# Sink-and-window attention with top-1 experts: packed score chunks, on-chip routing and 16 fixed expert blocks

## The chip, the cores and the metric

One core of one Trainium2 chip. The metric is device microseconds of one execution; the medians are over the runs shown. The profile is of one execution.

## The reference

Attention over 4 batches, 8 heads, 768 positions of 64 numbers. Heads 0, 2 and 6 (`retr` below) see all earlier positions, the other five ("streaming") the last 64 and the first 4 ("sinks"). The result, 3072 rows of 512, goes row by row through a layer of 8 experts: a row whose product with `w_skip` is positive goes to the expert with the largest logit, and its gated output is added to the row; every other row is left as it is.

```python
scores = np.where(mask[None, :, :, :], scores, -1000000000.0)
a = np.exp(scores - np.max(scores, axis=-1, keepdims=True))
attn = np.matmul(a / (np.sum(a, axis=-1, keepdims=True) + 1e-09), v)
...
do_compute = x @ w_skip > 0
e_idx = np.argmax(xc @ w_gate, axis=1)
h = np.maximum(xc[mask] @ w1[e], 0.0)
y[mask] = gate_w[mask, None] * (h @ w2[e])
out[do_compute] = xc + y
```

## The kernel before

It runs in four stages, and a framework orders each engine's instructions and sets the waits from what they read and write.

*Attention* (lines 162 to 327) loops over batches and pairs of heads. POOL's queue loads q, k and v head by head, cast to f16 on the way, in pieces of 64 numbers (lines 172, 174, 197). TensorE transposes q and k of a pair (lines 180, 184); ScalarE and VectorE copy them to `qT` and `kT`. Scores are computed transposed, keys on the partitions, 128 keys and up to 512 queries at a time with 64 rows of the array (line 217), into one PSUM bank of two; each goes through one exponential (line 223) and, where it touches a mask's edge, a VectorE product (lines 226, 249). A streaming head takes 128 keys by 256 queries, and its sinks are a strip of 4 rows. P·V (line 268) puts all six query tiles of a head in one PSUM tile, with a column of ones in V for the sum; lines 275 and 276 divide. After a batch the rows go to DRAM (`attn_x`), are transposed in fp32 (line 289), and multiplied by the gate's matrix (line 297); one row block of 128 at a time is turned into a gate weight and a one-hot row (lines 302 to 327).

*Routing* (lines 333 to 421) starts after the last batch: ranks by a triangular matmul, 24 indirect writes of row numbers to eight DRAM shards (line 404), a load of the shards, and a minimum over them.

*Experts* (lines 441 to 501): each expert has 384 slots, as 256 and 128, whatever its rows. Per expert POOL issues two weight loads, and per 128 slots a gather of rows (line 456) and of gate weights (line 463). VectorE scales, TensorE transposes in fp32 (line 472), then the up matmuls (line 481), one ReLU (line 488) and the down matmuls (line 493); the result goes to DRAM by slot.

*Return* (lines 503 to 518): per 128 rows an indirect load by slot (line 510), a sum and a store.

```python
          nc.gpsimd.dma_start(out=w1t, in_=w1r[e])
          nc.gpsimd.dma_start(out=w2t, in_=w2r[e])
          for mt in CHSZ:
            for s2 in range(nsm):
                nc.gpsimd.indirect_dma_start(
                    out=xg, out_offset=None, in_=X[:, :],
```

## Time and profile before

| | us |
|---|---|
| median of 3 runs (502.64 to 507.01) | 503.84 |
| profiled execution, first to last instruction | 499.5 |
| attention, 0 to 225 | 225 |
| routing, 225 to 281 | 56 |
| experts, 281 to 450 | 169 |
| return, 450 to 499.5 | 49.5 |

The profiled execution's own time is its span and the start and end around it, which the profile doesn't show; the median lies 4.3 us above the span. Engines are PE (TensorE), PEld (its weight loads), DVE (VectorE), ACT (ScalarE), POOL (GpSimd) and SP. A matmul's end is modelled; its start is recorded. The stages are told apart by which lines run.

### The profile page before, as it was taken

To read this page: it belongs to the slowest core of one execution; us is meant where nothing else is said; L and a number is where in the kernel's file an instruction comes from. 1 tells how busy PE (TensorE), PEld (TensorE's weight loads), DVE (VectorE), ACT (ScalarE), POOL (GpSimd) and SP (SyncE) were. 2 spreads that over 40 slices of the span, in tenths; PEclk is the share of its full clock that TensorE was granted. 3 is DMA by queue.
4 is the path that set the end of the run, shared out by engine and by line. 5 is a ranking of instruction groups with operands and counts; after the bars stand their busy time and mean duration, and the time that the engine had idled before them with its cause. 6 is when DMAs were issued, how large, how long until landed. Compare 5 with 4: busy or idle time off the path is not lost.

```text
span 499.5 us, 6050 instructions
## 1 busy us (share of the span) xinstructions
PE 313.7 (63%) x1981; PEld 175.0 (35%) x1981; DVE 208.8 (42%) x883; ACT 135.2 (27%) x317; POOL 202.8 (41%) x269
## 2 busy tenths in 40 slices
PE   0699999998999999962000048766868668770000
PEld 0344454444444444331000035534535444540000
DVE  1245566455654665467000134141441423316563
ACT  1464646564645564610000002101111012020000
POOL 9976751553011100000674636342533525005662
PEclk9999999999999999999999999979699798896555
DMA  4999991999132511031000694959679589512675
GB/s 31 120 103 88 82 202 11 70 65 173 11 25 18 142 10 8 2 126 2 1 0 9 112 206 112 170 126 206 122 162 168 122 162 183 125 52 95 211 229 184
DMA packets 108207, 50.51 MB, mean 101 GB/s; under 512 B 85079, under 2 KB 93671, under 8 KB 108176
## 3 DMA queue, kind: packets, MB, share of 16 engines
q0 software_dynamic: 94240, 31.04, 54.1%
q10 hardware_dynamic: 6000, 10.59, 6.0%
q1 hardware_dynamic: 7936, 8.51, 5.0%
q8 instruction: 15, 0.25, 0.2%
q14 instruction: 16, 0.13, 0.1%
HBM read 65.14 MB, written 19.00 MB: 168 GB/s over the span
## 4 chain that ended last, share of the span: by engine, by line
PE 45%; DMA 22%; issue 9%; POOL 9%; DVE 7%; ACT 6%; ACTq 0%; POOLq 0%; SPq 0%; DVEq 0%
DMA xg<-attn_x,merged 14%; PE pst L217 13%; PE opsa L268 10%; PE yps L493 6%; PE hps L481 5%; PE gxtp L289 4%; ACT ats L223 3%; ACT ht L488 2%; POOL fyg L510 2%; DMA fyg<-y_sorted,slot_i 2%; DMA gw<-gate_w,merged 2%; POOL sorted_sh L404 2%; PE qTps L180 2%; PE kTps L184 2%; DMA sorted_sh<-row_idx,slot_i 2%
## 5 line engine op out<-in xcount | busy, mean ns | idle before, releaser
L223 ACT ACTIVATE ats<-pst 128x256 f16<-128x256 f32 (+4 forms) x236 | 92.6, 417 | 74.1 <-PE pst L217 71.8
L217 PE MATMUL pst<-qT,kT 64*128 64x256 f16 (+4 forms) x236 | 91.0, 426 | 3.8 <-ACT ats L223 1.0
L488 ACT ACTIVATE ht<-hps 128x2048 f16<-128x2048 f32 (+1 forms) x16 | 23.2, 1450 | 196.8 <-PE hps L481 134.2
L268 PE MATMUL opsa<-va,ats 128*128 128x65 f16 x552 | 69.8, 241 | 2.9 <-ACT ats L223 2.3
L197 POOL DMA_DIRECT2D va<-in_v_dram x32 | 26.7, 843 | 94.0 <-PE opsa L268 54.5
L493 PE MATMUL yps<-w2t,ht 128*128 128x512 f16 x192 | 52.8, 433 | 18.7 <-ACT ht L488 18.7
L268 PEld LDWEIGHTS <-ats 128*128 128x128 f16 x552 | 41.3, 117 | 54.7 <-DVE ats L226 12.2
L481 PE MATMUL hps<-xTm,w1t 128*128 128x128 f16 (+1 forms) x512 | 48.0, 255 | 1.0 <-DVE xTm L475 1.0
L404 POOL DMA_INDIRECT sorted_sh<-row_idx,slot_i x24 | 23.4, 977 | 57.2 <-DVE slot_i L398 50.2
L481 PEld LDWEIGHTS <-w1t 128*128 128x128 f16 x512 | 42.0, 102 | 10.4 <-issue 3.8
L510 POOL DMA_INDIRECT fyg<-y_sorted,slot_i x24 | 26.5, 1104 | 42.2 <-DVE fyg L509 37.7
L472 PE MATMUL xtp<-identf,xg 128*128 128x128 f32 x96 | 18.9, 351 | 36.2 <-DVE xg L468 36.2
L468 DVE TENSOR_SCALAR xg<-xg,gw 128x512 f32<-128x512 f32 x24 | 11.4, 492 | 67.8 <-DMA xg<-attn_x,merged 52.2
L493 PEld LDWEIGHTS <-ht 128*128 128x128 f16 x192 | 19.2, 107 | 47.2 <-ACT ht L488 23.2
L456 POOL DMA_INDIRECT xg<-attn_x,merged x24 | 24.8, 1033 | 22.4 <-issue 19.0
L217 PEld LDWEIGHTS <-kT 64*128 64x128 f16 (+1 forms) x236 | 20.5, 102 | 27.8 <-issue 16.2
L289 PE MATMUL gxtp<-identf,xsb 128*128 128x128 f32 x96 | 29.3, 435 | 0.9 <-DVE xsb L276 0.9
L174 POOL DMA_DIRECT2D kin<-in_k_dram x32 | 27.8, 867 | 3.8 <-PE kTps L184 2.6
L172 POOL DMA_DIRECT2D qin<-in_q_dram x32 | 27.7, 866 | 3.0 <-PE pst L217 2.0
L475 DVE CAST xTm<-xtp 128x512 f16<-128x512 f32 x24 | 15.8, 681 | 30.7 <-PE xtp L472 30.7
L180 PE MATMUL qTps<-ident,qin 128*128 128x128 f16 x96 | 18.8, 308 | 14.9 <-DMA qin<-in_q_dram 14.9
L472 PEld LDWEIGHTS xtp<-identf,xg 128*128 128x128 f32 x96 | 14.7, 181 | 37.8 <-DVE xg L468 20.6
(111 smaller groups left out, 369.1 us busy)
## 6 DMA issues: line engine op xcount, KB each, us to landing
w1t<-in_moe_w_dram POOLq DMA_DIRECT2D x8, 1024.0 KB, 9.4
w2t<-in_moe_w_dram POOLq DMA_DIRECT2D x8, 1024.0 KB, 12.3
y_sorted<-ys ACTq DMA_DIRECT2D x16, 256.0 KB
qin<-in_q_dram POOLq DMA_DIRECT2D x32, 96.0 KB, 3.3
kin<-in_k_dram POOLq DMA_DIRECT2D x32, 96.0 KB, 3.3
va<-in_v_dram POOLq DMA_DIRECT2D x32, 96.0 KB, 3.2
attn_x<-xsb SPq DMA_DIRECT2D x12, 256.0 KB
attn_x<-xsb ACTq DMA_DIRECT2D x12, 256.0 KB
```

What stands on the lines that cost most here:

```text
L174: nc.gpsimd.dma_start(out=kin[:, :, hd, :], in_=kv[b, h0 + hd].transpose([1, 0, 2]))
L180: nc.tensor.matmul(qTps[:, n * P:(n + 1) * P], qin[:, n].rearrange("p h d -> p (h d)"), ident, is_transpose=True, start=(n == 0), stop=(n ...
L217: nc.tensor.matmul(pst[:k_rows, :qn], kTh[:, j * P:j * P + k_rows], qTh[:, q_lo:q_hi], start=True, stop=True)
L223: nc.scalar.activation(dst, pst[:k_rows, :qn], ACT.Exp)
L268: nc.tensor.matmul(opsa[:, i, :], ats[:kr, sl, i * QB:i * QB + QB], vh[:kr, j, :], start=(cnt == 1), stop=(cnt == total))
L289: nc.tensor.matmul(xtp[:, s, :], xc[:, s * P:(s + 1) * P], identf, is_transpose=True, start=(s == 0), stop=(s == DS - 1))
L404: nc.gpsimd.indirect_dma_start(out=SH[c % NSHARD][:, None], out_offset=bass.IndirectOffsetOnAxis(ap=slot_i[:, c:c + 1], axis=0), in_=row_i ...
L472: nc.tensor.matmul(xtp[:, s, :], xg[:, s * P:(s + 1) * P], identf, is_transpose=True, start=(s == 0), stop=(s == DS - 1))
L481: nc.tensor.matmul(hps[:, fs, :mt], w1t[:, s, fs * P:(fs + 1) * P], xT[:, s, :mt], start=(s == 0 and fs % BPB == 0), stop=(s == DS - 1 and ...
L488: nc.scalar.activation(ht[:, :, :mt], hps[:, :, :mt], ACT.Relu)
L493: nc.tensor.matmul(yps, ht[:, fs, s2 * P:(s2 + 1) * P], w2t[:, fs, :], start=(fs == 0), stop=(fs == FS - 1))
L510: nc.gpsimd.indirect_dma_start(out=yg, out_offset=None, in_=YS[:, :], in_offset=bass.IndirectOffsetOnAxis(ap=slot_i[:, c:c + 1], axis=0), ...
```

## The change

The kernel is written anew. What it does:

- q and k are loaded whole per batch (only batch 0 in parts), 384 numbers a piece, so position 6p + n lies on partition p; v by tiles of 128 positions. All of it is issued by POOL, and so are the weights: batches 0 and 1 and expert 0 at the start, then one batch and one expert a round, with buffers for five experts.
- `trans` transposes each head apart, onto output rows 0 to 63 or 64 to 127. `retr` packs the lower triangle of a retrieval head into three chunks of up to 1024 columns, each with one exponential. `strm` packs a streaming head's window into one tile of 768 columns, keys 0 to 63 of each tile on the upper half and 64 to 127 on the lower, the lower shifted by 64. `sinks` computes the sink scores of five heads in one tile of 20 rows.
- `prep_v` copies V on POOL so that the shifted tiles find theirs. `avx` does P·V for one query tile of all heads, divides, stores the rows to the output itself, and makes the logits from an f16 cast by POOL.
- The scores of batch b stand beside `avx` of batch b - 1, one query tile at a time (`front`, `NF` and the loop at line 486).
- `route` turns a batch's logits into ranks, and by one-hot matmuls into a table with row number and gate of each of 256 slots of each expert, without DRAM; the gate is carried in three f16 parts.
- The experts have 2 blocks of 128 slots. All 16 gathers read the output, up to 128 rows each; the result is added to the gathered rows and scattered back to the output (line 581). After that the largest count is read into the engines' registers; if it is over 256, a loop does the further blocks with weights loaded again (lines 604 to 671).

```diff
+    def load_qk(b, split):
+        q_in[b] = qkp.tile([P, H, NT * D], FP16, tag="qin", name="qin")
...
+    def load_v(b):
+        va[b] = vp.tile([P, NT, H, V1], FP16, tag="va", name="va")
+        for i in range(NT):
+            nc.gpsimd.dma_start(out=va[b][:, i, :, :D], in_=vr[b, i])
...
+    load_qk(0, True)
+    load_v(0)
...
+    load_qk(1, False)
+    load_v(1)
+    load_w(0)
...
+    sp = att.enter_context(tc.tile_pool(name="sp", bufs=2, space=PSUM))
+    tp = att.enter_context(tc.tile_pool(name="tp", bufs=2, space=PSUM))
+    ap_ = att.enter_context(tc.tile_pool(name="ap", bufs=1, space=PSUM))
...
+    def prep_v(b):
+        nc.gpsimd.memset(va[b][:, :, :, D:], 1.0)
+        vs[b] = vsp.tile([P, NT, 5, V1], FP16, tag="vs", name="vs")
+        for dst, src in ((slice(0, 4), slice(1, 8, 2)), (slice(4, 5), slice(4, 5))):
+            nc.gpsimd.tensor_copy(vs[b][:D, :, dst], va[b][:D, :, src])
+            nc.gpsimd.tensor_copy(vs[b][D:, 1:, dst], va[b][D:, :NT - 1, src])
...
+    def trans(b, pr):
+        for name, src, dst in (("qT", q_in[b], qT), ("kT", k_in[b], kT)):
+            ps = tp.tile([P, NT, P], FP16, tag="t", name="tps")
+            for n in range(NT):
+                for i, h in enumerate(PAIRS[pr]):
+                    nc.tensor.matmul(ps[i * D:(i + 1) * D, n],
+                                     src[:, h, n * D:(n + 1) * D], ident,
+                                     is_transpose=True, start=(n == 0),
+                                     stop=(n == NT - 1))
...
+    CH = (((0, 0, 0, 512), (0, 512, 512, 256), (4, 512, 768, 256)),
+          ((1, 128, 0, 512), (1, 640, 512, 128), (3, 384, 640, 384)),
+          ((2, 256, 0, 512), (5, 640, 512, 128)))
+    CHO = ((0, 1024, 768), (1024, 1024, 640), (2048, 640, 512))
...
+        for j, q0, o, w in CH[c]:
+            for i in heads:
+                r = slice(i * D, (i + 1) * D)
+                nc.tensor.matmul(ps[i][:, o:o + w], kT[b, pr][r, j * P:(j + 1) * P],
+                                 qT[b, pr][r, q0:q0 + w], start=True, stop=True)
...
+    def strm(b, pr, i):
...
+        ps = sp.tile([P, 1024], FP32, tag="s", name="sps")
+        for n in range(NT):
+            c = n * P
+            nc.tensor.matmul(ps[:D, c:c + P], kt[r, c:c + D], qt[r, c:c + P],
+                             start=True, stop=True)
+            lo, hi = (0 if n == 0 else c + D), min(c + D + P, S)
+            for x, y in (((lo, 512), (512, hi)) if lo < 512 < hi else ((lo, hi),)):
+                nc.tensor.matmul(ps[D:, x:y], kt[r, c + D:c + P], qt[r, x:y],
+                                 start=True, stop=True)
...
+        nc.scalar.activation(a, ps[:, :S], ACT.Exp, scale=SCALE)
+        nc.vector.tensor_tensor(a, a, smask.rearrange("p i c -> p (i c)"), op=ALU.mult)
...
+    def avx(b, i):
...
+        x = xp.tile([P, 4, 2, D], FP32, tag="x", name="x")
+        for t in range(2):
+            o = ap_.tile([P, 4, V1], FP32, tag=f"av{t}", name=f"av{t}")
+            nc.tensor.matmul(o, esk[b % 2][:, i * P:(i + 1) * P], vsk[:, b, t],
+                             start=True, stop=False)
+            for c in range(4):
+                h = 2 * c + t
+                a = at[b, h]
+                fin = c == 3
+                if h in RETR:
+                    for j in range(i + 1):
+                        x0 = COL[j] + (i - j) * P
+                        nc.tensor.matmul(o[:, c], a[:, x0:x0 + P], va[b][:, j, h],
+                                         start=False, stop=fin and j == i)
+                else:
+                    u = SINKS.index(h) if h != 4 else 4
+                    q0 = i * P
+                    nc.tensor.matmul(o[:D, c], a[:, q0:q0 + D], vs[b][:, i, u],
+                                     start=False, stop=fin)
+                    nc.tensor.matmul(o[D:, c], a[:, q0 + D:q0 + P], va[b][:, i, h],
+                                     start=False, stop=fin)
+            rec = tiny.tile([P, 4], FP32, tag=f"rec{t}", name="rec")
+            nc.vector.reciprocal(rec, o[:, :, D])
+            nc.vector.tensor_tensor(x[:, :, t], o[:, :, :D],
+                                    rec.unsqueeze(2).to_broadcast([P, 4, D]), op=ALU.mult)
+        xf = x.rearrange("p c t d -> p (c t d)")
+        (nc.sync if i % 2 else nc.scalar).dma_start(out=outr[b, i], in_=xf)
+        x16 = xp.tile([P, DM], FP16, tag="x16", name="x16", bufs=2)
...
+    def route(b):
...
+        for i in range(NT):
+            ol = tiny.tile([P, P], FP16, tag="ol", name="ol", bufs=4)
+            nc.vector.tensor_scalar(ol, iota16, lo[:, i:i + 1], None, ALU.is_equal)
+            nc.tensor.matmul(tb, ol, mv[:, i], start=(i == 0), stop=(i == NT - 1))
...
+    for b in range(B + 1):
+        steps = list(front(b)) if b < B else []
+        if b < B:
+            prep_v(b)
+        for i in range(NT):
+            if b:
+                avx(b - 1, i)
+            for f in steps[i * len(steps) // NT:(i + 1) * len(steps) // NT]:
+                f()
+        if b:
+            route(b - 1)
+        if b + 2 < B:
+            load_qk(b + 2, False)
+            load_v(b + 2)
+        if b + 1 < NW and b < B:
+            load_w(b + 1)
+    att.close()
...
+        def gather(e):
...
+                sl = t * E + e
+                xg[e, t] = mxp.tile([P, DM], FP32, name=f"xg{e}_{t}")
+                nc.vector.memset(xg[e, t], 0.0)
+                nc.gpsimd.indirect_dma_start(
+                    out=xg[e, t], out_offset=None, in_=out[:, :],
+                    in_offset=bass.IndirectOffsetOnAxis(ap=idx[:, sl:sl + 1], axis=0),
+                    bounds_check=N - 1, oob_is_err=False)
+        for e in range(3):
+            gather(e)
+        load_w(NW)
+        for e in range(3, E):
+            gather(e)
+        for e in range(NW + 1, E):
+            load_w(e)
...
+        def down(e):
...
+                sl = t * E + e
+                yp = myp.tile([P, DM], FP32, tag="my", name="myp")
+                for f in range(FS):
+                    nc.tensor.matmul(yp, hts[e][:, f, t * P:(t + 1) * P], w2t[:, f],
...
+                nc.vector.scalar_tensor_tensor(xg[e, t], yp, gs[:, sl:sl + 1], xg[e, t],
+                                               ALU.mult, ALU.add)
+                nc.gpsimd.indirect_dma_start(
+                    out=out[:, :],
+                    out_offset=bass.IndirectOffsetOnAxis(ap=idx[:, sl:sl + 1], axis=0),
+                    in_=xg[e, t], in_offset=None, bounds_check=N - 1, oob_is_err=False)
+        up_(0)
+        for e in range(E):
+            if e + 1 < E:
+                up_(e + 1)
+            down(e)
...
+    most = nc.values_load(cnt_i[:1, E:E + 1], min_val=0, max_val=N)
+    with tc.If(most > T2 * P), \
...
-            nc.gpsimd.indirect_dma_start(
-                out=SH[c % NSHARD][:, None],
-                out_offset=bass.IndirectOffsetOnAxis(ap=slot_i[:, c:c + 1],
-                                                     axis=0),
...
                 nc.gpsimd.indirect_dma_start(
-                    out=xg, out_offset=None, in_=X[:, :],
-                    in_offset=bass.IndirectOffsetOnAxis(
-                        ap=idxs[:, s2:s2 + 1], axis=0),
...
-                nc.gpsimd.indirect_dma_start(
-                    out=yg, out_offset=None, in_=YS[:, :],
-                    in_offset=bass.IndirectOffsetOnAxis(
-                        ap=slot_i[:, c:c + 1], axis=0),```

How the framework orders it, at three places. First POOL, in attention. Before (`va`: a head's V, `gw` and `row_idx`: of the routing):

```order
L356 IOTA e_rep_i_3173 1x192
L401 IOTA row_idx_3203 128x24
L462 MEMSET gw_3324 128x1
L462 MEMSET gw_3341 128x1
L462 MEMSET gw_3418 128x1
L462 MEMSET gw_3487 128x1
L197 DMA va_1336<-in_v_dram 128x6x64
L197 DMA va_1339<-in_v_dram 128x6x64
L197 DMA va_1666<-in_v_dram 128x6x64
```

Now, where batch 2 begins (`va_484`: V of batch 2, `vs_1142`: its copy, `x16`: the cast rows of batch 1):

```order
L277 COPY skq1_130<-kT_926 64x4 x2
L102 DMA qin_1126<-in_q_dram 128x8x384
L103 DMA kin_1127<-in_k_dram 128x8x384
L249 MEMSET va_484 128x48
L368 CAST x16_1174<-x_1149 128x512
L253 COPY vs_1142<-va_484 64x6x260
L254 COPY vs_1142<-va_484 64x5x260
L253 COPY vs_1142<-va_484 64x6x65
L254 COPY vs_1142<-va_484 64x5x65
L368 CAST x16_1262<-x_1234 128x512
L114 DMA w1t_2409<-in_moe_w1_dram 128x4x1024
```

Before, POOL had loads and no work that attention waits for; now the memset and the copies of batch 2's V, which wait for its load, stand ahead of the casts of batch 1's rows.

Then TensorE, in P·V. Before (`ats`: a head's exponentials, `pst`: scores):

```order
L268 LDWEIGHTS ats_520
L268 MATMUL opsa_553<-va_465,ats_520 128x65
L217 LDWEIGHTS kT_459
L217 MATMUL pst_550<-qT_458,kT_459 4x512
L217 LDWEIGHTS kT_593
L217 MATMUL pst_603<-qT_592,kT_593 128x512
```

Now (`atr`: a retrieval head, `ats`: a streaming head, `esk`: the sinks):

```order
L352 LDWEIGHTS atr_306
L352 MATMUL av0_685<-va_85,atr_306 128x65
L343 LDWEIGHTS esk0_131
L343 MATMUL av1_701<-vsk_128,esk0_131 128x260
L357 LDWEIGHTS ats_418
L357 MATMUL av1_701<-vs_201,ats_418 64x65
L359 LDWEIGHTS ats_418
L359 MATMUL av1_701<-va_85,ats_418 64x65
```

A streaming head's P·V is now two matmuls of 64 output rows each, and one sink matmul of 260 columns stands for four heads.

Last POOL, in the experts. Before (`xg`: gathered rows, `gw`: gathered gate weights):

```order
L444 DMA w1t_3314<-in_moe_w1_dram 128x4x1024
L445 DMA w2t_3315<-in_moe_w2_dram 128x8x512
L456 DMA xg_3319<-attn_x,merged_96 128x512
L463 DMA gw_3324<-gate_w,merged_96 128x1
L456 DMA xg_3336<-attn_x,merged_96 128x512
L463 DMA gw_3341<-gate_w,merged_96 128x1
L456 DMA xg_3413<-attn_x,merged_96 128x512
L463 DMA gw_3418<-gate_w,merged_96 128x1
L444 DMA w1t_3477<-in_moe_w1_dram 128x4x1024
L445 DMA w2t_3478<-in_moe_w2_dram 128x8x512
```

Now (`xg6_0` is the first block of expert 6; the blocks of experts 0 to 4 stand ahead in the same way):

```order
L530 DMA xg5_0_2853<-out_0_dram,idx_2794 128x512
L530 DMA xg5_1_2858<-out_0_dram,idx_2794 128x512
L530 DMA xg6_0_2863<-out_0_dram,idx_2794 128x512
L114 DMA w1t_2829<-in_moe_w1_dram 128x4x1024
L530 DMA xg6_1_2868<-out_0_dram,idx_2794 128x512
L530 DMA xg7_0_2873<-out_0_dram,idx_2794 128x512
L530 DMA xg7_1_2878<-out_0_dram,idx_2794 128x512
L114 DMA w1t_2883<-in_moe_w1_dram 128x4x1024
L116 DMA w2t_2831<-in_moe_w2_dram 128x8x512
L581 DMA out_0_dram<-xg0_0_2799,idx_2794 3072x512
```

Weights no longer stand between gathers, but for one load of expert 5; the scatters follow when all gathers are issued.

## Rows read from the trace of the kernel before

**Rows 1.** The page's first line.

```profile
span 499.5 us, 6050 instructions
```

**Rows 2.** Busy us (instructions) of PE, PEld, DVE, ACT, POOL by stage; clock, DMA share, GB/s.

```profile
0.00:225.00 225.00, 194.03 (x1168) 97.07 (x1168) 117.97 (x685) 111.45 (x299) 87.10 (x137) 1.00 0.75 71
225.00:281.00 56.00, 3.92 (x13) 2.08 (x13) 11.93 (x58) 0.55 (x4) 26.26 (x27) 1.00 0.07 6
281.00:450.00 169.00, 115.80 (x800) 75.89 (x800) 51.52 (x94) 23.20 (x16) 62.91 (x81) 0.89 0.74 149
450.00:499.50 49.50, 0.00 (x0) 0.00 (x0) 27.41 (x48) 0.00 (x0) 26.50 (x24) 0.54 0.57 181
```

**Rows 3.** The chain that ended last, in the experts: start, us, what.

```profile
315.60 13.32 DMA xg<-attn_x,merged
...
337.94 12.82 DMA xg<-attn_x,merged
```

**Rows 4.** Timeline of PE in attention: start, us, line, operation, shapes, how many.

```profile
87.86 0.59 PE L268 MATMUL opsa<-va,ats 128*128 128x65 f16 x7
...
88.39 0.61 PE L217 MATMUL pst<-qT,kT 64*128 64x256 f16 x2
88.93 0.40 PE L180 MATMUL qTps<-ident,qin 128*128 128x128 f16 x2
89.11 0.63 PE L184 MATMUL kTps<-ident,kin 128*128 128x128 f16 x4
...
98.11 1.39 PE L268 MATMUL opsa<-va,ats 4*128 4x65 f16 x10
```

**Rows 5.** Groups by line and shape, PE: busy us, mean ns, idle before.

```profile
L268 PE MATMUL opsa<-va,ats 128*128 128x65 f16 x472 | 59.6, 242 | 0.0
...
L217 PE MATMUL pst<-qT,kT 64*128 64x256 f16 x124 | 43.7, 391 | 2.2 <-ACT ats L223 0.8
...
L184 PE MATMUL kTps<-ident,kin 128*128 128x128 f16 x96 | 16.9, 307 | 0.4 <-DMA kin<-in_k_dram 0.4
```

**Rows 6.** Timeline of PE in the experts.

```profile
334.87 3.66 PE L481 MATMUL hps<-xTm,w1t 128*128 128x256 f16 x32
...
340.56 3.63 PE L493 MATMUL yps<-w2t,ht 128*128 128x512 f16 x16 [1.59 <-ACT ht L488]
...
447.25 1.90 PE L493 MATMUL yps<-w2t,ht 128*128 128x512 f16 x8 [1.18 <-ACT ht L488]
```

**Rows 7.** Groups by line and shape, ACT and DVE.

```profile
L488 ACT ACTIVATE ht<-hps 128x1024 f16<-128x1024 f32 x8 | 8.2, 1023 | 73.7 <-DVE xg L468 62.6 <-PE hps L481 11.1
...
L190 ACT ACTIVATE qT<-qTps 128x768 f16<-128x768 f16 x16 | 12.9, 805 | 11.4 <-PE qTps L180 11.4
...
L276 DVE TENSOR_TENSOR xsb<-opsa,rec 128x384 f32<-128x384 f32 x32 | 17.8, 556 | 0.3
...
L191 DVE COPY kT<-kTps 128x768 f16<-128x768 f16 x16 | 8.8, 552 | 3.4 <-PE kTps L184 1.9 <-PE pst L217 1.4
...
L324 DVE TENSOR_SCALAR ef<-ef 128x1 f32<-128x1 f32 x24 | 3.5, 146 | 0.0
```

**Rows 8.** Groups by line and shape, POOL.

```profile
L174 POOL DMA_DIRECT2D kin<-in_k_dram x32 | 27.8, 867 | 3.8 <-PE kTps L184 2.6 <-PE pst L217 1.2
...
L456 POOL DMA_INDIRECT xg<-attn_x,merged x24 | 24.8, 1033 | 22.4 <-issue 19.0 <-DVE xTm L475 3.5
...
L120 POOL TENSOR_SCALAR_AFFINE_SELECT retr_diag<-retr_diag 128x128 f16<-128x128 f16 x1 | 0.3, 315 | 0.0
```

**Rows 9.** DMA: POOL's queue (packets, MB, share), issues to landing (us); last line of 456.

```profile
q0 software_dynamic: 94240, 31.04, 54.1%
...
w1t<-in_moe_w_dram POOLq DMA_DIRECT2D x8, 1024.0 KB, 9.4
w2t<-in_moe_w_dram POOLq DMA_DIRECT2D x8, 1024.0 KB, 12.3
...
DMA to landing us min/median/max: 2.1/10.1/14.1
```

More of the change, by code (lines that the diff above doesn't have):

```diff
@@ L16 @@
 ACT = mybir.ActivationFunctionType
+PSUM = bass.MemoryType.PSUM
 B = 4
@@ L24 @@
 WINDOW = 64
-IS_RETR = [1, 0, 1, 0, 0, 0, 1, 0]
+P = 128
+NT = S // P
 N = B * S
@@ L30 @@
 F = 1024
-QB = 128
-NQB = S // QB
-P = 128
-MTOK = 256
-ECAP = MTOK + P
+DS = DM // P
+FS = F // P
+V1 = D + 1
+RETR = (0, 2, 6)
+PAIRS = ((0, 2), (4, 6), (1, 3), (5, 7))
+SINKS = (1, 3, 5, 7, 4)
+COL = {0: 0, 4: 768, 1: 1024, 3: 1664, 2: 2048, 5: 2560}
+RW = 2688
+SCALE = 1.0 / D ** 0.5
+T2 = 2
+NSLOT = T2 * E
+BIG = 1 << 16
+TOK0 = N // 2
+NW = 5
 @with_exitstack
@@ new lines @@
+    nc.gpsimd.affine_select(
+        out=mid, in_=mid, compare_op=ALU.is_ge, fill=0.0,
+        base=WINDOW - 1, pattern=[[0, 5], [-1, P]], channel_multiplier=1)
+    last = up[D:, D + 5 * P:]
+    nc.gpsimd.affine_select(
+        out=last, in_=last, compare_op=ALU.is_ge, fill=0.0,
+        base=0, pattern=[[1, D]], channel_multiplier=-1)
+    NR = 4 * len(SINKS)
+    vraw = const.tile([NR, B, V1], FP16, name="vraw")
+    nc.vector.memset(vraw, 1.0)
+    for i, h in enumerate(SINKS):
+        nc.gpsimd.dma_start(
+            out=vraw[4 * i:4 * i + 4, :, :D],
+            in_=v[:, h, :N_SINK, :].rearrange("b k d -> k b d"))
@@ new lines @@
+    vsk = const.tile([NR, B, 2, 4, V1], FP16, name="vsk")
+    skq = [const.tile([P, 3, NR], FP16, name=f"skq{i}") for i in range(2)]
+    esk = [const.tile([NR, S], FP16, name=f"esk{i}") for i in range(2)]
+    for t_ in skq:
+        nc.vector.memset(t_, 0.0)
+    for t_ in esk:
+        nc.vector.memset(t_, 0.0)
+    iota_i = const.tile([P, P], I32, name="iota_i")
+    nc.gpsimd.iota(iota_i, pattern=[[1, P]], base=0, channel_multiplier=0)
+    iota16 = const.tile([P, P], FP16, name="iota16")
@@ new lines @@
+    nc.vector.tensor_copy(iota16, iota_i)
+    rev_i = const.tile([P, NT, E], I32, name="rev_i")
+    nc.gpsimd.iota(rev_i, pattern=[[0, NT], [-1, E]], base=E, channel_multiplier=0)
+    rev = const.tile([P, NT, E], FP32, name="rev")
+    nc.vector.tensor_copy(rev, rev_i)
+    tok_i = const.tile([P, B * NT], I32, name="tok_i")
+    nc.gpsimd.iota(tok_i, pattern=[[P, B * NT]], base=-TOK0, channel_multiplier=1)
+    vals = rt.tile([P, B * NT, 4], FP16, name="vals")
+    nc.vector.tensor_copy(vals[:, :, 0], tok_i)
@@ new lines, in trans @@
+    def trans(b, pr):
[7 more added lines that the diff above has]
+                                     stop=(n == NT - 1))
+            t = qtp.tile([P, S], FP16, tag=name, name=name)
+            o = t.rearrange("c (p n) -> c n p", n=NT)
+            if ev[0] % 2:
+                nc.scalar.copy(o, ps)
+            else:
+                nc.vector.tensor_copy(o, ps)
+            ev[0] += 1
+            dst[b, pr] = t
+        for i, h in enumerate(PAIRS[pr]):
+            if h in SINKS:
+                s_ = SINKS.index(h)
+                nc.gpsimd.tensor_copy(
+                    skq[b % 2][i * D:(i + 1) * D, max(pr - 1, 0), 4 * s_:4 * s_ + 4],
+                    kT[b, pr][i * D:(i + 1) * D, :N_SINK])
@@ new lines, in front @@
+    def front(b):
+        yield lambda: trans(b, 0)
+        for c in range(3):
+            yield lambda c=c: retr(b, 0, (0, 1), c)
+            if c == 0:
+                yield lambda: trans(b, 1)
+        yield lambda: retr(b, 1, (1,), 0)
+        yield lambda: trans(b, 2)
+        yield lambda: retr(b, 1, (1,), 1)
+        yield lambda: retr(b, 1, (1,), 2)
+        yield lambda: strm(b, 1, 0)
+        yield lambda: trans(b, 3)
+        yield lambda: strm(b, 2, 0)
+        yield lambda: strm(b, 2, 1)
+        yield lambda: strm(b, 3, 0)
+        yield lambda: strm(b, 3, 1)
+        yield lambda: sinks(b)
```

722 lines of the change are left out of this document (327 added, 395 removed).

## The prediction

> **What bounds the kernel now.** I read the page's first line, the busy times by stage, the chain that ended last, and then single stretches of TensorE's timeline. The span is 499.5 us [rows 1], and four stages follow each other [rows 2]. Attention takes 225 us: TensorE has a matmul in flight for 194 of them, VectorE is busy for 118 and ScalarE for 111, at a granted clock of 1.00, so TensorE sets the pace; its 1168 matmuls come 0.193 us apart on average. Routing takes 56 us in which no engine works for more than 26: it is trips through DRAM. The experts take 169 us; the chain of waits there is a row of gathers that take about 13 us each [rows 3], because the indirect loads stand in one queue behind 4 MB of weights, and the granted clock falls to 0.89. The last 49.5 us bring rows back from DRAM, with TensorE idle.
>
> What one matmul costs is read from starts, since ends are modelled: a run's length less the mean of its last one [rows 5], over the number of gaps [rows 4]. Seven P·V matmuls of one shape: (0.59 - 0.24) / 6 = 0.058 us. Ten P·V of which some have 4 rows: (1.39 - 0.24) / 9 = 0.128. Four f16 transposes: (0.63 - 0.31) / 3 = 0.107. Two score matmuls with 64 rows and 256 columns take 88.93 - 88.39 = 0.54, so 0.27 each and about 1 ns a column, the weight load in it; I take 0.86, since the first of the two starts the second after 0.22. The experts' matmuls [rows 6]: with 256 columns 3.66 / 32 = 0.114, the last one's end in it; with 512 columns, by the difference of 16 and 8 of them, (3.63 - 1.90) / 8 = 0.216.
>
> **The change, part by part.** The new kernel removes both DRAM trips of the routing, a third of the expert blocks (16 for 24) and the final gather; it keeps the attention's arithmetic but cuts it into other tiles.
>
> *Start, 45 us to the first P·V that needs V.* POOL issues every load. Ahead of the V copies (line 249) stand 33 issues of 0.867 us [rows 8] = 28.6, some 20 mask and iota instructions (0.315 for 128 elements, up to six times as wide: 8 us in all), and the four copies of up to 1560 elements a lane, which no row shows: 1.3 us in all if each costs what 128 elements do, 11 if it scales; I take 4.5, nearer the first, which is what the row itself shows. The issues of batch 1's loads and of the first weights also wait for an earlier load to land; 4 us for that. Together 45 (35 to 55). The scores of batch 0 lie inside it.
>
> *Attention, three rounds of scores of batch b beside P·V of batch b-1.* TensorE per round: 96 transposes onto 64 output rows, 10.3 us at 0.107, 5.2 if the two halves of a pair overlap, take 8; 24 score matmuls of the retrieval heads with 8064 columns, 6.9 at 0.86 ns, 4.6 if heads overlap, take 5.8; 65 small ones of the streaming heads with 7680 columns, 3.3 if halves overlap, 14.3 at 0.22 each (what a 128-column one would take before another shape), take 8; sinks 1.7; P·V of retrieval heads 63 x 0.058 = 3.7; of streaming heads 60, also 3.5, between 2 and 7.7 (0.128 each); 12 sink matmuls of 260 columns, 3; 36 changes between shapes at 0.11 ((0.128 - 0.058) x 9 / 6, six changes in that run), 4.1; 24 transposes of x in f16, 2.6; logits and ranks 1.7. Sum 42 (29.5 to 56.6). Beside it lie ScalarE, 6 instructions of 1.02 us and 19 of 0.8 or less = 21, and VectorE, 12 of at most 0.56, 9 of 0.55 and some 62 of about 0.2 = 24 [rows 7]; both fit under 42. Against the four rounds of 56 us before (225 / 4) a round falls by 14.
>
> POOL is in order, and the copies of V for batches 2 and 3 stand there ahead of the casts that TensorE's x transposes wait for. They wait for a V load that can be issued only when the old buffer's last P·V is done, and that lies behind weights in the queue: a pair lands 13.2 us after its first issue (0.9 + 12.3) [rows 9]. I take 5 us each (0 to 20): 10. Then batch 3's P·V alone, the last seven terms: 18.
>
> *Routing after the last batch, 10 us.* Batches 0 to 2 are routed beside attention. For the last one some 30 VectorE instructions of 0.15 to 0.2 us run one after another with two trips to TensorE, and memsets of the gather targets stand between them; 6 to 15.
>
> *Experts, 72 us.* All 16 gathers stand ahead of all but one of the late weights, five of eight experts' weights are long there, so a gather should land in the 2.1 us that is the least before, not in the median of 10.1 [rows 9]: 1.0 issue + 2.1 + cast, transposes and copy 2.5 = 6. Then TensorE per expert: 32 x 0.114 + 8 x 0.107 + 16 x 0.216 = 8.0; eight of them 64; 2 more because the clock has fallen in the pause. The gathers come at 2.1 us an expert, faster than they are used, and weights 5 to 7 are issued 12 us or more before they are needed. Evacuation, 4 instructions of at most 0.8 us on ScalarE and 6 of about 0.6 on VectorE an expert [rows 7], is hidden under 8.0.
>
> *Tail, 8 us:* the last combine 0.7, scatter issue 1.0, landing 3.5, loading the largest count into the engines' registers and the jump over the overflow code about 2 to 3; no row shows a jump, 0 to 8.
>
> Sum: 45 + 3 x 42 + 10 + 18 + 10 + 72 + 8 = 289 us of span. The median of the runs shown is 503.84, 4.3 above the profiled span, so **293**.
>
> **A rule weighed.** The run in which 4-row matmuls are mixed in shows 0.128 us a matmul against 0.058 for one shape [rows 4]. The Trainium skill (TensorEngine Tiling (Array Packing), Key Properties) says that a change of the tiling mode drains the engine while different tiles of one mode run in parallel. The first half agrees with 0.128 against 0.058 and speaks against a kernel with more shapes: without the 36 changes a round would be 38 us instead of 42, and with the last batch's P·V the whole 277. The second half no row here shows; it is the first rival below.
>
> **Rivals.**
> - *The halves overlap.* Transposes, streaming scores and streaming P·V use 64 output rows each and alternate between two halves. If alternate halves run side by side, a round is 29.5 us and VectorE's 24 is close behind: 45 + 3 x 31 + 5 + 15 + 10 + 70 + 8 + 4 = 250. For it: they have different output rows and weights. Against: nothing in this trace alternates halves of the output rows.
> - *POOL's queue bounds.* A round issues some 10 loads and a pair of weights in order with casts and copies; if each round waits for its V load and one pair, 13 us, it is 55 us: 45 + 3 x 55 + 18 + 10 + 72 + 8 + 4 = 322. For it: POOL's one queue carries loads, weights, gathers and the casts; against: there are five weight buffers, and q and k come in pieces six times as long as before.
> - *Matmuls stay 0.193 us apart.* 388 a round give 75: 45 + 225 + 35 + 10 + 72 + 8 + 4 = 399. For it: more shapes and single buffers for the P·V results. Against: the dear 64-row scores become fewer and the sink strips of 4 rows go.
> - *Slower than before: the overflow code runs.* If one expert holds more than 256 rows, all eight pairs of weights are loaded again, 8 x 13.2 = 106 us with nothing beside them, and each further block costs a gather, up and down with nothing beside them, about 20 us as between the gathers at 315.60 and 337.94 [rows 3]. It is slower than before from 6 further blocks: 293 + 106 + 6 x 20 = 519. That would be so if most of the 3072 rows were routed (384 an expert). Against: POOL's queue carried 31.04 MB [rows 9]; q, k and v are 9.44 (96 loads of 96 KB) and the weights 16.78 (16 of 1024 KB), so 4.82 are left for gathering each routed row twice, 2 KB each, some 1,180 rows or 147 an expert.
>
> **How the numbers follow.** Forecast 0.66, overlap 0.11, POOL's queue 0.13, unchanged spacing 0.07, overflow code 0.03 (half of it below 504). The forecast's own bounds by the terms above: 35 to 55 for the start, 30 to 57 for a round, 6 to 15, 0 to 40 for the waits; taken together 260 to 335. The range goes to 250 for the overlap and to 350 for the queue. A measurement tells about 1% from no change; by these cases faster has 0.97, same 0.01, slower 0.02.
>
> **What would show it.** The first P·V after 40 to 50 us; rounds of about 42 us with TensorE busy throughout at clock 1.00; POOL's casts of x late once or twice, behind the copies of V; no gather over 4 us; expert matmuls in one dense stretch of 64 us; no instruction of the overflow code. Rounds over 50 us with TensorE idle would make the queue right, rounds of 75 with it busy the unchanged spacing, and rounds near 30 the overlap.

## The result and the profile after

The changed kernel takes 318.34 us (median of 4 runs, 318.25 to 318.79) against 503.67 for the one before in the same comparison: a ratio of 0.632, with a 95% interval of 0.630 to 0.634. Forecast were 293 us. The direction and the range held; 25 us are missing, and they are in one place.

First the page of the changed kernel, as [rows 1] before: the span, the busy time of TensorE (PE) in 40 slices, and the granted clock.

```profile
span 316.6 us, 5049 instructions
...
PE   0148589798755999668998897116999999930000
...
PEclk9999999999999999999999999999999999985555
```

The last four slices have no TensorE work and about 30 us of span. The stages show it in time; columns as in [rows 2], six of the eleven stretches.

```profile
45.00:88.10 43.10, 35.80 (x381) 22.36 (x380) 24.33 (x61) 26.56 (x27) 19.51 (x33) 1.00 1.23 222
88.10:134.80 46.70, 35.94 (x380) 22.04 (x381) 26.74 (x72) 26.36 (x26) 19.29 (x30) 1.00 1.23 165
134.80:180.20 45.40, 37.61 (x395) 23.02 (x394) 29.22 (x89) 26.59 (x26) 7.27 (x15) 1.00 0.10 36
...
217.90:280.10 62.20, 61.14 (x440) 41.17 (x437) 27.03 (x44) 17.16 (x30) 23.30 (x24) 1.00 0.78 149
280.10:309.90 29.80, 0.05 (x2) 0.00 (x0) 1.17 (x5) 0.00 (x0) 8.84 (x9) 0.54 0.12 44
309.90:316.60 6.70, 0.00 (x0) 0.00 (x0) 0.00 (x0) 0.00 (x0) 0.00 (x0) 0.50 0.02 7
```

Put beside the terms of the forecast:

| stage | forecast, us | after, us |
|---|---|---|
| start, scores of batch 0 | 45 | 45.0 |
| three rounds and POOL's waits | 126 + 10 | 135.2 |
| last batch's P·V | 18 | 19.1 |
| routing of the last batch | 10 | 10.6 |
| first gather to first up matmul | 6 | 8.0 |
| expert matmuls | 64 + 2 | 62.2 |
| tail | 8 | 36.5 |
| outside the span | 4.3 | 1.7 |

The first row runs to the last score matmul of batch 0; the first P·V with V, which the forecast's 45 meant, starts at 41.1. Seven terms are right to 4 us, and together too long by 3.5; the tail is 28.5 too short. The chain that ended last begins at 289.8 us, before which it isn't followed, and is one thing only: a scatter's landing, the issue of the next, its landing.

```profile
299.19 2.53 DMA out_dram<-xg,idx
...
301.76 0.51 issue
...
302.49 2.10 DMA out_dram<-xg,idx
```

POOL's timeline shows where this row of scatters came from (start, us, engine, line, operation, and in brackets the idle time ahead of it).

```profile
233.42 0.98 POOL L116 DMA_DIRECT2D w2t<-in_moe_w_dram  x1
237.97 1.07 POOL L581 DMA_INDIRECT out_dram<-xg,idx  x1 [3.56 <-DVE xg L579]
239.02 0.91 POOL L114 DMA_DIRECT2D w1t<-in_moe_w_dram  x1
...
249.05 1.05 POOL L581 DMA_INDIRECT out_dram<-xg,idx  x1 [8.23 <-DMA out_dram<-xg,idx]
259.29 1.03 POOL L581 DMA_INDIRECT out_dram<-xg,idx  x1 [9.19 <-DMA out_dram<-xg,idx]
260.30 0.97 POOL L116 DMA_DIRECT2D w2t<-in_moe_w_dram  x1
263.07 1.01 POOL L581 DMA_INDIRECT out_dram<-xg,idx  x1 [1.79 <-DVE mx L550]
271.73 0.98 POOL L581 DMA_INDIRECT out_dram<-xg,idx  x1 [7.65 <-issue]
...
308.88 0.98 POOL L581 DMA_INDIRECT out_dram<-xg,idx  x1 [2.54 <-DMA out_dram<-xg,idx]
```

All 16 scatters (line 581) write the same DRAM tensor, and each is issued only when the one before has landed. In the chain a scatter lands 2.1 to 2.8 us after the start of its issue, and the next issue follows 0.8 us later: from 271.73 to 308.88 eleven steps in 37.2 us, 3.4 each. The first four took 11.1, 10.2, 3.8 and 8.7 us to the next, because weights of experts 5 to 7 (lines 114 and 116) stand in the same queue ahead of their data; that this is the cause, and not only the order, is tested below. So the chain, which in the best case is 16 x 3.4 = 54 us, no longer than the 62 us of matmuls, began late and stretched, and its last scatter was issued 29 us past the last matmul. The Trainium skill (DMA: Bandwidth & Descriptors, Two DMAs through the same engine are not ordered) says that standing in the same queue orders no writes, and that the dependent DMA has to wait on the first one's semaphore. The trace agrees as to the wait: the second scatter was issued 11 us after the first, though both are in one queue. What would come without the wait no run shows.

The attention has its length for other reasons than forecast. TensorE is in flight for 36 us of a round, not 42, and 7 to 11 us of a round are pauses. The longest of them on TensorE's timeline, and then a tile of q, one of k and some P·V without a pause:

```profile
91.19 0.64 PE L452 MATMUL tbp<-mv,ol 128*128 128x64 f16 x4
96.34 0.40 PE L371 MATMUL tps<-ident,x 128*128 128x128 f16 x2 [4.51 <-POOL x L368]
```

```profile
153.27 0.85 PE L262 MATMUL tps<-ident,qin 128*64 128x128 f16 x12
153.91 0.85 PE L262 MATMUL tps<-ident,kin 128*64 128x128 f16 x12
...
155.33 0.24 PE L352 MATMUL av<-va,atr 128*128 128x65 f16 x1
155.50 0.40 PE L343 MATMUL av<-vsk,esk 20*128 20x260 f16 x1
155.82 0.26 PE L357 MATMUL av<-vs,ats 128*64 128x65 f16 x1
155.83 0.26 PE L359 MATMUL av<-va,ats 128*64 128x65 f16 x1
```

The 4.51 us are a wait for a cast of x that stands on POOL behind the preparation of V. The transposes onto 64 output rows start a tile of 12 every 0.64 us (153.27, 153.91), 0.053 each, half of the 0.107 that one of 128 rows takes in [rows 4]: the two halves run side by side, which an experiment below takes up. The two kinds of streaming P·V (lines 357 and 359) start together as well. A change of shape costs 0.17 us to the next start (155.33, 155.50) against 0.054 within a shape, the 0.11 of the forecast.

The groups by shape show what the forecast had missed beside TensorE:

```profile
L271 DVE COPY qT<-tps 128x768 f16<-128x768 f16 x16 | 43.5, 2720 | 17.5 <-PE tps L262 17.1
L269 ACT COPY kT<-tps 128x768 f16<-128x768 f16 x16 | 43.5, 2716 | 26.5 <-PE tps L262 26.5
```

The copies of q and k took 0.805 and 0.552 us in the kernel before [rows 7]; they now take 2.72. The tile is as large, but the output is written with a step of 12 bytes (every sixth column), to undo the order in which the new loads bring the tokens.

### The profile page after: what moved, and what is told of

It reads as the page before. It is cut to its first block, busy times and chain, and to the rows that moved or that the text cites. A ratio compares the mean times of both kernels' runs of the same rounds, so it can differ in the third digit from the quotient of the medians.

```text
span 316.6 us, 5049 instructions
## 1 busy us (share of the span) xinstructions
PE 209.7 (66%) x1996; PEld 133.7 (42%) x1996; DVE 153.5 (48%) x406; ACT 124.7 (39%) x137; POOL 126.2 (40%) x190
## 2 busy tenths in 40 slices
PE   0148589798755999668998897116999999930000
## 5 line engine op out<-in xcount | busy, mean ns | idle before, releaser
L269 ACT COPY kT<-tps 128x768 f16<-128x768 f16 x16 | 43.5, 2716 | 26.5 <-PE tps L262 26.5
L271 DVE COPY qT<-tps 128x768 f16<-128x768 f16 x16 | 43.5, 2720 | 17.5 <-PE tps L262 17.1
L301 ACT ACTIVATE atr<-sps 128x1024 f16<-128x1024 f32 (+1 forms) x36 | 32.9, 948 | 17.7 <-PE sps L296 17.6
L581 POOL DMA_INDIRECT out_dram<-xg,idx x16 | 15.9, 997 | 56.8 <-DMA out_dram<-xg,idx 34.4
L368 POOL CAST x<-x 128x512 f16<-128x512 f32 x24 | 15.0, 627 | 43.0 <-DVE x L363 23.5
L562 PE MATMUL mhp<-mxT,w1t 128*128 128x256 f16 x256 | 30.8, 281 | 1.1 <-ACT mxT L555 0.4
L577 PE MATMUL myp<-w2t,ht 128*128 128x512 f16 x128 | 29.9, 379 | 0.0
L296 PE MATMUL sps<-qT,kT 64*128 64x512 f16 (+3 forms) x96 | 28.3, 474 | 2.0 <-ACT kT L269 2.0
L374 ACT COPY xT<-tps 128x512 f16<-128x512 f16 x24 | 14.1, 588 | 39.0 <-PE tps L371 19.4
L562 PEld LDWEIGHTS <-w1t 128*128 128x128 f16 x256 | 25.8, 101 | 7.3 <-issue 2.8
L371 PE MATMUL tps<-ident,x 128*128 128x128 f16 x96 | 15.2, 302 | 19.1 <-DVE qT L271 12.3
L352 PE MATMUL av<-va,atr 128*128 128x65 f16 x252 | 24.9, 243 | 0.0
L262 PE MATMUL tps<-ident,qin 128*64 128x128 f16 x192 | 13.7, 312 | 15.6 <-POOL ident masks.py:199 13.4
L530 POOL DMA_INDIRECT xg<-out_dram,idx x16 | 16.5, 1029 | 17.4 <-DVE idx L516 12.8
L555 ACT COPY mxT<-mtp 128x512 f16<-128x512 f16 x16 | 8.7, 588 | 35.5 <-PE mtp L553 35.5
L566 DVE TENSOR_SCALAR ht<-mhp 128x512 f16<-128x512 f32 x16 | 11.1, 692 | 23.7 <-PE mhp L562 23.7
L343 PE MATMUL av<-vsk,esk 20*128 20x260 f16 x48 | 18.8, 394 | 2.9 <-DVE x L363 1.7
L363 DVE TENSOR_TENSOR x<-av,rec 128x256 f32<-128x256 f32 x48 | 19.9, 420 | 1.6
L352 PEld LDWEIGHTS <-atr 128*128 128x128 f16 x252 | 15.9, 123 | 9.5 <-issue 7.6
L357 PE MATMUL av<-vs,ats 128*64 128x65 f16 x120 | 19.4, 254 | 0.7 <-DVE ats L324 0.7
## 6 DMA issues: line engine op xcount, KB each, us to landing
w1t<-in_moe_w_dram POOLq DMA_DIRECT2D x8, 1024.0 KB, 14.2
w2t<-in_moe_w_dram POOLq DMA_DIRECT2D x8, 1024.0 KB, 15.9
va<-in_v_dram POOLq DMA_DIRECT2D x24, 128.0 KB, 10.1
kin<-in_k_dram POOLq DMA_DIRECT2D x3, 768.0 KB, 17.1
```

The source lines that it names most:

```text
L269: nc.scalar.copy(o, ps)
L271: nc.vector.tensor_copy(o, ps)
L296: nc.tensor.matmul(ps[i][:, o:o + w], kT[b, pr][r, j * P:(j + 1) * P], qT[b, pr][r, q0:q0 + w], start=True, stop=True)
L301: nc.scalar.activation(a[:, o:o + w], ps[i][:, :w], ACT.Exp, scale=SCALE)
L343: nc.tensor.matmul(o, esk[b % 2][:, i * P:(i + 1) * P], vsk[:, b, t], start=True, stop=False)
L352: nc.tensor.matmul(o[:, c], a[:, x0:x0 + P], va[b][:, j, h], start=False, stop=fin and j == i)
```

## The experiments

All go back to the changed kernel (318.3 us); where two edits stand in one kernel, the text says so. Each was timed in 2 runs unless said otherwise.

### The tail: is it the chain, the weights, or the transfers?

**Own targets.** Each scatter gets a DRAM tensor of its own, so that nothing has to land before the next is issued.

```diff
+ own = nc.dram_tensor(f"own{sl}", (N, DM), FP32, kind="Internal").ap()
- out=out[:, :],
+ out=own[:, :],
```

> Each of the 16 scatters writes into a DRAM tensor of its own, so none has to wait until the one before it has landed; the output lacks the experts' share. Theory (chain): in the changed kernel a scatter is issued only when the one before has landed, 3.3 us each at the end, and the last 8 are issued after the experts' last combine at 280.9 us; without the chain the last is issued by 282.5 and lands by 285, so the 25 us behind it go: time about 293 us (290 to 297). Rival (transfer): the scatters need their 3 us each in the queue whether or not they wait for each other: time stays at 312 to 318. Rival (weights alone): the late weights in the same queue hold the scatters up, and the waiting for each other costs nothing: time stays within 3 us of 318.

Measured: 291.55 us (291.38 to 291.72). POOL's timeline at the end:

```profile
278.51 0.98 POOL L582 DMA_INDIRECT own<-xg,idx  x1 [0.74 <-DVE xg L579]
280.23 0.98 POOL L582 DMA_INDIRECT own<-xg,idx  x1 [0.74 <-DVE cmx L599]
```

The last scatter is issued at 280.2, right behind its combine, and the weights are where they were. Transfers and weights alone are out; the waiting for each other is needed for the tail.

**No late weights.** The chain stays, but experts 5 to 7 use the tiles of experts 0 to 2.

```diff
- load_w(NW)
  for e in range(3, E):
      gather(e)
- for e in range(NW + 1, E):
-     load_w(e)
+ for e in range(NW, E):
+     wts[e] = wts[e - NW]
```

> Experts 5 to 7 use the weights of experts 0 to 2, so no weights are loaded while the experts run; the chain of scatters stays. This leaves out the right weights of three experts. Theory (chain, made late by weights): the first scatters took 11, 10, 4 and 9 us from issue to issue because 6 MB of weights stood in the queue; without them the chain starts when the last gather has landed, at about 233, and is 16 x 3.3 = 53 us long: last issue at about 285, time about 295 us (291 to 300). Rival (chain alone): the chain by itself is what makes the tail, and the time falls by less than 8 us, to 310 or more. Rival (weights alone): the scatters keep up with the experts, last issue at 282, time 292.

Measured: 295.54 us (295.37 to 295.71).

```profile
234.43 1.04 POOL L580 DMA_INDIRECT out_dram<-xg,idx  x1 [3.11 <-DVE ht L565]
237.89 1.00 POOL L580 DMA_INDIRECT out_dram<-xg,idx  x1 [2.41 <-DMA out_dram<-xg,idx]
...
286.89 0.98 POOL L580 DMA_INDIRECT out_dram<-xg,idx  x1 [3.79 <-DMA out_dram<-xg,idx]
```

16 scatters from 234.4 to 286.9, 3.5 each, as the theory has it. So either cause taken away gives 23 to 27 us back: the long tail needs both. With the chain alone the last scatter is issued 7 us after the last matmul (279.9), and the program takes 4.0 us more than with the weights alone; a kernel without both was not tried.

**Weights early.** A version that leaves nothing out: three of the six late pieces go into the space of q and k (the pool that is closed) as soon as batch 3's transposes are done, three into the attention's space at its end.

```diff
+ if b == B - 1 and i == 4:
+     late.close()
+     load_w(NW, w5)
+     w6a = load_w1(NW + 1, w5, "w6a")
...
+ wts[NW + 1] = w6a, load_w2(NW + 1, w7, "w6b")
+ load_w(NW + 2, w7)
```

> Three of the six late weight pieces are loaded into the space of q and k once batch 3's transposes are done, the other three into the space of the attention's tiles as soon as it ends, all ahead of the gathers; nothing else differs from the changed kernel and nothing is left out. Theory (chain, made late by weights): no weights stand in front of a scatter, so the chain starts at about 235 and takes 53 us; the first gather may be 1 to 5 us later because of the last weights: time about 297 us (293 to 301). Rival (the weights are only moved in front of the gathers): the first gather lands over 8 us later and the gain is under 12 us, 306 or more.

Measured: 299.15 us (297.68 and 300.62), 19 less. The chain runs from 234.1 to 289.7; the first up matmul starts at 221.4 in place of 217.9, the 3.5 us that the last weights cost the gathers.

### The copies of q and k

**Swapped walk**: the same copy, with the tokens in the inner loop, so that writes are contiguous and reads step 256 bytes through PSUM.

```diff
- o = t.rearrange("c (p n) -> c n p", n=NT)
+ o = t.rearrange("c (p n) -> c p n", n=NT)
+ pi = ps.rearrange("c n p -> c p n")
- nc.scalar.copy(o, ps)
+ nc.scalar.copy(o, pi)
```

> The 32 copies of transposed q and k walk their 768 elements in the other order: reads step 256 bytes through PSUM, writes are contiguous (before: reads contiguous, writes step 12 bytes). Same result. Theory (strided writes): a copy falls from 2.72 us to near the 0.83 us that an activation of 768 elements takes, and the waits of TensorE on these copies (about 5 us a round, and most of the idle 11 us of the first front) go: time about 300 us (294 to 308). Rival (any stride costs): copies stay over 2 us, time within 2 us of 318. Rival (TensorE paces the rounds): copies fall, the time by less than 5 us.

**Flat**: both sides contiguous, the tokens left in the loads' order.

```diff
- o = t.rearrange("c (p n) -> c n p", n=NT)
+ o = t.rearrange("c (n p) -> c n p", n=NT)
```

> The copies of q and k leave the columns in the order of the transposes, so reads and writes are both contiguous; the tokens of q and k then stand in another order and the attention weights are other ones. Theory (strided writes): this is the floor for the copies, 0.6 to 0.9 us each on both engines, and the time about 300 us, like the copy with strided reads or up to 3 us below it. Rival (TensorE paces the rounds): time over 313.

Measured: 310.86 us (310.73 to 310.98) and 304.66 (302.90 and 306.41). The copies on VectorE and ScalarE, swapped:

```profile
L272 DVE COPY qT<-tps 128x768 f16<-128x768 f16 x16 | 15.3, 957 | 17.4 <-PE tps L262 17.1
...
L270 ACT COPY kT<-tps 128x768 f16<-128x768 f16 x16 | 12.8, 799 | 26.4 <-PE tps L262 26.4
```

and VectorE's flat:

```profile
L271 DVE COPY qT<-tps 128x768 f16<-128x768 f16 x16 | 8.9, 556 | 16.9 <-PE tps L262 16.9
```

So the step in the writes costs ScalarE 1.9 us a copy and VectorE 2.2 (2.72 against 0.556); the step in the PSUM reads costs ScalarE nothing and VectorE 0.4. The Trainium skill (SBUF — State Buffer, in the section Door 1) says that SBUF is served in lines of 16 bytes and that a walk which goes to a new line each time pays; at a step of 12 bytes three of four elements are on a new line, and the trace agrees with 2.72 against 0.80 us for 768 elements, at the one step that was run.

The theory was right on the copies and not on the time: 7.5 us gained, not 18. (Of the flat kernel's 13.7 some 8 are another matter: its third round took 32 us, with P·V matmuls 0.03 to 0.04 apart in place of 0.054; see the last section.) By the ends of the sinks' matmuls the third round fell from 45.3 to 40.4 us, the first two only from 42.6 and 46.7 to 42.3 and 44.2. What holds them shows in the waits of TensorE from 86 to 130 us of the swapped kernel (us in total, times, longest):

```profile
PE tps L372 <- POOL x L369: 7.4, 2, 5.8
```

### POOL's order

**Casts on ScalarE**: with the swapped walk, the casts of x and the small copies for the sinks leave POOL.

```diff
- nc.gpsimd.tensor_copy(x16, xf)
+ nc.scalar.copy(x16, xf)
- nc.gpsimd.tensor_copy(
+ nc.scalar.copy(
      skq[b % 2][i * D:(i + 1) * D, max(pr - 1, 0), 4 * s_:4 * s_ + 4],
```

> The swapped walk of the q and k copies (310.9 us alone) and, in addition, the casts of x and the copies for the sinks on ScalarE in place of POOL. Theory (POOL's queue): with short copies two of three rounds still took 42 to 44 us because TensorE waited 4.9 and 7.4 us for casts that stand on POOL behind V copies and V loads that wait for their data or for a weight transfer; the third round, without loads on POOL, went from 45 to 40. With the casts elsewhere these waits go: about 299 us (295 to 303). Rival (TensorE paces the rounds): under 4 us gained, 307 or more. Rival (ScalarE becomes late, 24 casts of about 0.6 us more): between 303 and 312 with waits of TensorE on ScalarE.

Measured: 299.94 us (298.67 and 301.22), 10.9 less than the swapped walk alone. The three rounds:

```profile
35.90:77.40 41.50, 35.63 (x385) 22.38 (x387) 17.83 (x56) 23.33 (x37) 21.11 (x29) 0.50 1.50 212
77.40:118.70 41.30, 36.56 (x389) 22.31 (x390) 22.39 (x79) 23.18 (x37) 13.60 (x19) 0.50 1.34 218
118.70:159.50 40.80, 36.63 (x390) 22.42 (x391) 22.06 (x79) 23.18 (x37) 4.42 (x5) 0.50 0.37 68
```

They are now even, 41 us with TensorE in flight for 36. Most of the gain is not in them: the first front (batch 0's scores) ends at 35.9 us in place of 43.6, since the last matmuls of a front wait for the small copies, which on POOL stood behind V. The expectation hit the time and not the place: it counted on the waits of two rounds, and the three rounds together became only 3 us shorter (126.8 to 123.6).

**Earlier start**: in addition the identity is built ahead of the loads, and batch 0's V is prepared ahead of batch 1's loads.

> As the kernel with short copies and casts on ScalarE, and the identity is built ahead of the first loads and batch 0's V is prepared ahead of batch 1's loads. Theory (POOL's order sets the start): TensorE starts its first transposes when the first q and k land, at 5 to 7 us, in place of 13.4, and the first P·V comes at about 30 in place of 41; time 8 to 11 us under the one without it. Rival (the loads pace the start): batch 1's q, k and V, issued later, come late for the second front, and less than 4 us are gained.

Measured: 294.83 us (294.71 to 294.96), 5.1 less. TensorE starts at 4.2 us in place of 13.5 and the first P·V comes at 28.2; the front ends at 31.3. Half of the forecast gain: it was counted from a first P·V at 41, and with the short copies and the casts on ScalarE that stood at 36.6 already.

### Do halves of the output rows overlap?

The transposes of a tile in another order, first all six of one half, then the other.

```diff
- for n in range(NT):
-     for i, h in enumerate(PAIRS[pr]):
+ for i, h in enumerate(PAIRS[pr]):
+     for n in range(NT):
```

> The changed kernel with the 12 transposes of a tile of q or k in another order: first the six onto output rows 0 to 63, then the six onto 64 to 127, in place of alternating. Theory (halves overlap): in the changed kernel a pair starts together and pairs are 0.106 us apart, so 12 take 0.64 us; on one half alone they come 0.106 each, 12 take 1.28 us, 20 us more TensorE time over 32 tiles, of which the pauses of TensorE hide a part: time 323 to 335 us. Rival (pairs only look simultaneous, the modelled starts deceive): 12 still take 0.64, time within 2 us of 318.

Measured: 325.06 us (324.27 and 325.84), inside the theory's range, but not for its reason:

```profile
153.42 0.85 PE L262 MATMUL tps<-ident,qin 128*64 128x128 f16 x10
154.06 0.31 PE L262 MATMUL tps<-ident,kin 128*64 128x128 f16 x1
154.06 0.31 PE L262 MATMUL tps<-ident,qin 128*64 128x128 f16 x1
```

The next tile starts 0.64 us after this one, as before, so that the edit did not part the halves. Yet the single starts show what it was to show. Of q's tile and the k's behind it, the first two transposes stand alone and are 0.11 us apart (153.42 and 153.52), and so do the last two (154.70 and 154.81); all between them start in pairs, a pair every 0.107 us. On one half alone a transpose takes 0.107 us, and where both halves have work two start together. So the rival's reading doesn't hold. The order in the program does not decide which stand beside each other; what does, no run shows.

The attention is 0.7 us longer; the rest lies in the experts, which take 8 us more: TensorE stands still for nearly 6 us in front of the second expert's up matmuls, and the 32 of them take 5.9 us in place of 3.7.

```profile
223.82 1.03 PE L577 MATMUL myp<-w2t,ht 128*128 128x512 f16 x4
230.67 5.54 PE L562 MATMUL mhp<-mxT,w1t 128*128 128x256 f16 x29 [5.83 <-ACT mxT L555]
```

ScalarE and VectorE took up the first expert's last results 3 to 5 us later than in the changed kernel, without a cause that the profile names. A like pause stands in the profiles of the last two kernels below, and in no other. These three ran on another chip than the other eight, so that the chip is not ruled out, though the kernel before takes the same time on both (504.9 us, and 504.8 to 505.2). It stays open.

### Together

All four edits (swapped walk, casts, start, weights), 4 runs:

> All four: short copies, casts on ScalarE, the earlier start, the weights ahead of the gathers. If the parts add: 318 - 7.5 - 12 - 9 - 22 = 268 us (260 to 275). Under 258 would say that TensorE, with fewer pauses, also ran parts of the attention at the higher of its two clocks, as the kernel with contiguous copies did from 140 to 160 us (P·V matmuls 37 ns apart instead of 54). Over 278 would say that two parts give the same time back.

Measured: 273.08 us (273.01 to 274.06); its ratio to the kernel before is 0.542 (0.539 to 0.544). That is 45 us below the changed kernel; the parts, each in its own comparison, give 7.5 + 10.9 + 5.1 + 19.2 = 42.7.

```profile
31.30:72.60 41.30, 35.41 (x373) 21.70 (x373) 17.76 (x51) 23.36 (x37) 17.45 (x22) 1.00 1.54 205
72.60:114.40 41.80, 31.47 (x397) 20.39 (x396) 25.50 (x84) 23.03 (x37) 19.45 (x26) 0.88 1.36 216
114.40:154.40 40.00, 36.48 (x389) 22.43 (x390) 21.85 (x83) 23.18 (x37) 6.86 (x10) 0.50 0.69 137
...
256.10:272.10 16.00, 0.01 (x2) 0.00 (x0) 1.17 (x5) 0.00 (x0) 2.15 (x3) 0.57 0.08 24
```

Three rounds and the tail: of 36.5 us behind the last matmul 16 are left.

**Routing in pieces**, 4 runs, and the same **without the overflow code**, 4 runs:

```diff
+ if b > 1 and i in (1, 3):
+     next(parts, None)
```

> The kernel with all four edits (273.1 us), and the routing of a batch cut into three pieces that are emitted between the tiles of the next round, so that TensorE meets the rank and table matmuls after VectorE has done what they need. Theory: TensorE waited 2.9, 2.6 and 0.3 us for them at 72 to 79 us and 0.6 at 116; these go, 6 us less: 266 to 268 us; if the denser work makes TensorE rise to its higher clock earlier or longer than from 85 to 105 us, down to 255. Rival (the waits only hide others): 271 to 274.

> The same without the overflow code: the test of the largest count, the jump and the loops are left out, so experts with more than 256 rows would lose the rest. It prices the jump: after the last scatter the program takes 7 us to its end. Theory (the jump is on the path): 2 to 4 us less than the kernel with it. Rival (the landing of the last scatter hides it): within 1 us of it.

Measured: 272.56 us (267.76 to 275.86) and 271.56 (268.83 to 278.81). The runs lie too far apart for a verdict on either. In both profiles TensorE's waits for the rank and table matmuls (2.8 and 2.6 us around 75) are gone, and one of 2.9 or 3.4 us for VectorE's division stands in their place. The last P·V comes at 166.1 us in the first profile, its longest run, and at 170.1 in the second, whose attention is the same, against 170.8 in the kernel with four edits; so no gain can be credited to the edit. The experts of both have the pause above.

Of the overflow code only this is shown: after the start of the last scatter the program ends after 5.4 us without it (265.5 to 270.9), and with it after 9.3 in the kernel with all four edits (262.8 to 272.1), 7.7 in the changed kernel and 7.0 in the one without late weights. Its test and jump cost 1.6 to 3.9 us by these.

## Why the prediction was right, and where not

**The step that failed** is "Tail, 8 us: the last combine 0.7, scatter issue 1.0, landing 3.5", and the jump. It priced one scatter, the last. The sum had no term for the other 15: that each waits for the landing of the one before was in the kernel (one output tensor, rows known only at run time), and 1.0 and 3.5 stood in the same sentence; 16 x 4.5 = 72 us against 64 of matmuls would have shown that the chain has to be priced. Measured it is 3.5 a scatter, 52 us from first to last issue, and as it can begin only with the first expert's result (234.4) it ends after the matmuls even without the weights. And the forecast took the late weights as harmless because they are issued 12 us before they are needed; they are not late for the matmuls, but they stand ahead of the scatters. The two runs that take away one or the other (291.6 and 295.5) both land on the forecast of 293, so the rest of the sum came out right.

**Start, 45 us**: right in its working for POOL. The copies of V take 4.6 us (4.5 forecast), the waits ahead of them 4.4 (4), and they run until 41.8; the sinks' small copies, which had no term, run until 43.4 and the front ends at 44.7. The first P·V, at 41.1, did not wait for POOL: it starts when the last scores before it are done, and these were held up by the long copies. With short copies the first P·V moves to 37.2 and does wait for POOL, and the front ends at 43.6 still; with work taken from POOL it ends at 35.9, then 31.3. So two paths ended within 4 us of each other, and the forecast had one. TensorE's wait of 13.4 us for the identity had not been seen; what it alone costs no run shows.

**Rounds, 42 us and 10 of POOL's waits**: right as a sum by luck, with errors in its parts that cancel. TensorE needs 36, not 42: transposes 96 x 0.053 = 5.1 in place of 8, and the streaming heads' matmuls run in pairs. That was the first rival's mechanism; it was given 0.11 because nothing in the trace of before alternated halves, and it is there. Its time of 250 did not come. Its 29.5 us a round supposed TensorE 6 us shorter than it is, and ScalarE and VectorE hidden; they were busy for 24 to 29 of 45 us, their copies at 2.72 us, where the forecast had taken 0.805 and 0.552 from rows of the same size but with contiguous writes. The copies and POOL's work account for 4 of the 9 us a round between 36 and 45; the other 5 are still there with both gone (41 us, 36 in flight) and were not taken apart. The bounds of a round, 29.5 to 56.6, are not the sums of the terms beside them either: these give 31.9 and 56.0.

**POOL's casts late behind V**: right once of twice. One wait of 4.51 us at 91.8, where two of 5 had been taken; for batch 3's V TensorE has no such wait. With the swapped walk, where the copies are short, it is 7.4 us of waits in that round. It never set a round of 55 us.

**Last P·V, 18**: measured 19.1; the "last seven terms" add up to 20.3.

**Routing 10, experts 72**: 10.6 and 70.2. The gathers land in 3.6 us (median; at most 7.6, where none over 4 was expected), where 2.1 had been taken, and the matmuls took 62.2 in place of 64 + 2.

**Unchanged spacing** and **overflow code** did not come: POOL jumps over the loops, at 1.6 to 3.9 us, inside the 0 to 8.

**The rule weighed** in the prediction: both of its halves are in the trace, with 0.11 us more at a change of shape and 0.053 us a transpose. The forecast had used the first and left the second to a rival.

## What to carry to other kernels

Price a DMA that repeats as a chain before pricing it as a last event: the time from one issue over its landing to the next issue, times its number, counted from when the first can start, against the work that is to hide it; and ask what else stands in its queue. A copy's price is that of its access pattern and not of its size: look at the step of the writes before taking the row of an old copy. A sum that comes out right can hold two errors; only the stage table and the busy time in each stage tell.
